# Gated layer, second pass: block sums move from GpSimd to VectorE, and one of them into the first pass

## The chip, the cores and the metric

One core of one Trainium2 chip. The time is the device time of one execution of the whole kernel in microseconds (us); lower is better. The engines are TensorE (PE in the rows; PEld is its weight load), VectorE (DVE), ScalarE (ACT), GpSimd (POOL) and SyncE (SP), which issues most of the DMAs.

## The reference, cut to what matters

Linear attention over 8 batches of 576 tokens gives a table of 4608 tokens by 512 features. A mixture of experts (one expert per token) works on it, and then the gated layer, which is the part that the change touches:

```python
rms = np.sqrt(np.mean(x * x, axis=-1, keepdims=True) + 1e-06)
xn = x / rms * rms_g                      # 4608 x 512
g = xn @ w_gate                           # 512 x 1536
silu = g * (1.0 / (1.0 + np.exp(-g)))
val = xn @ w_val                          # 512 x 1536
return (silu * val @ w_out).astype(np.float32)   # w_out: 1536 x 512
```

## The kernel before

The kernel runs attention, routing, experts and the gated layer one after the other, with some overlap. Only the gated layer matters here. It works on nine groups `j` of 512 tokens, in two passes, and each matrix product is done on 2x2 blocks with seven block products instead of eight (Strassen's scheme in Winograd's form); values are split into an upper and a lower half in 16 bits, and each block product is three 16-bit products.

**First pass** (`gated`, the loop over `j`). It computes u = silu(g) * val, transposed, and stores it to a scratch tensor `uscr` in DRAM as four blocks of 1536 columns for each group. Group 0 is computed plainly, in twelve chunks of features (`gate_chunk`: L1462 and L1463 make the product, L1465 stores it). Groups 1 to 8 go by `gate_group(j, i, more)`, three parts `i` each. A part makes seven block products for the gate (m = 0) and then seven for the value (m = 1), 12 matmuls each. In m = 1, `last` multiplies a block of the value by the finished block of the gate on VectorE (L1433) and issues its store on SyncE (L1434); the four blocks come in the order (2,2), (1,1), (2,1), (1,2). Between products, `more()` places pieces of the next group's preparation in program order: `in_gather` (four indirect DMAs issued by GpSimd, L1237), `in_rows` (the norm), `in_blocks` (four differences of blocks on GpSimd, L1291, splits on ScalarE and VectorE, L1300 and L1301, and transposes issued by SyncE, L1302). During group 0 the sums of the gate and value weights are made too (`all_sums`: VectorE L1347, GpSimd L1348 to L1351).

**Second pass** (`out_group(j)`). `out_load(j)` fetches the four blocks of u of a group from `uscr` into `ob[j % 2]` (768 KB each, SyncE). From them come the left operands of seven block products. Each operand is made by `out_left(j, n)`: ScalarE writes its upper 16-bit half (L1523) and VectorE the lower one (L1524), into one of five slots `os`. Four of the operands need sums of blocks, written in place by `out_sum`: t2 = t0 - t2 and t3 = t3 - t2 and t0 = t3 + t0 on GpSimd (L1511, L1513, L1515) and t1 = t1 - t3 on VectorE (L1517). `ahead(j, n)`, called behind product n, makes the operand of product n + 4, which may be one of the next group; with it come the sums that this operand or a later one needs, and behind operand 6 the loads of group j + 2.

`mul(n, p, first)` is one block product, 36 matmuls of 256 columns (L1557). The products 0 to 6 go into the PSUM banks a, d, g, b, e, a, e: product 6 adds onto bank e, which product 4 filled and which VectorE must have read before (L1572, the scaled add in `res` with u3). The results are added up with scaled adds on VectorE (L1589, L1590, L1572) and two scaled copies on ScalarE (L1582, L1596) and written out by `put`, four scatters of rows per group, indirect DMAs of GpSimd (L1575). The last of them, `left_put`, is issued in the next group.

All engines work their instructions in program order; the order is written out by hand, without a planner, in this part. At the junction of the passes, operands 0 and 1 of group 0 are made during group 8's last part; the slots 2 to 4 and `ob[1]` lie in memory that the first pass uses until its last store.

Of the kernel before, what the change touches and what calls it, by code (L numbers as in the profile page):

```python
# [9 lines left out]
F32 = mybir.dt.float32  # L10
# [6 lines left out]
ALU = mybir.AluOpType  # L17
# [6 lines left out]
NT, DM = B * S, H * D  # L24
# [109 lines left out]
class Kern:  # L134
# [1261 lines left out]
    def gate_group(self, j, i, more):  # L1396

        nc, v = self.nc, self.nc.vector
        x = self.xnT[j]

        def mul(p, k, r, first):
            n = 0
            for q in range(2):
                for dcl in range(2):
                    for w, y in ((0, 0), (0, 1), (1, 0)):
                        c = (y * 2 + dcl) * 256
                        nc.tensor.matmul(p[:, q * 256 : q * 256 + 256], self.left(k, self.m_, i, q, dcl, w), x[:, r, c : c + 256], start=first and n == 0, stop=n == 11, skip_group_check=True)  # L1407
                        n += 1

        out = {}  # L1410
        for m in range(2):
            self.m_ = m
            a, b, c, d = (self.ps.tile([128, 512], F32, tag="hy"[m], bufs=4, name=f"p{'abcd'[t]}{j}_{i}{m}") for t in range(4))
            mul(a, 0, 0, True)
            s1 = self.tmp(f"s{j}{i}{m}")
            nc.scalar.activation(s1, a, AF.Copy)  # L1416
            mul(b, 4, 1, True)
            u2 = self.tmp(f"u2{j}{i}{m}")
            v.tensor_tensor(u2, b, s1, ALU.add)
            mul(c, 5, 2, True)  # L1420
            u3 = self.tmp(f"u3{j}{i}{m}")
            v.tensor_tensor(u3, c, u2, ALU.add)
            mul(d, 3, 3, True)
            v.tensor_tensor(u3, d, u3, ALU.add)  # L1424
            c21 = self.tmp(f"c{j}{i}{m}")
            if m == 0:
                def last(o, t, key):
                    nc.scalar.activation(o, t, AF.Silu, scale=self.cg.bitcast(F32))  # L1428
                    out[key] = o
            else:  # L1430
                def last(o, t, key):
                    u, (r, h) = out[key], key
                    v.scalar_tensor_tensor(u, t, self.cv.bitcast(F32), u, ALU.mult, ALU.mult)  # L1433
                    nc.sync.dma_start(self.uscr[j, :, 2 * h + r - 3, i * 512 : i * 512 + 512], u)  # L1434

            last(u3, u3, (2, 2))
            more()
            mul(a, 1, 4, False)
            last(s1, a, (1, 1))
            more()  # L1440
            mul(c, 2, 5, False)
            v.tensor_tensor(c21, c, u2, ALU.add)  # L1442
            last(c21, c21, (2, 1))
            more()
            mul(d, 6, 6, False)
            v.tensor_tensor(u2, d, u2, ALU.add)
            last(u2, u2, (1, 2))

    def gate_chunk(self, j, fc):
        nc, v = self.nc, self.nc.vector  # L1450
        xT = self.xnT[j].rearrange("p a b -> p (a b)")[:, 0:4096].rearrange("p (c t) -> p c t", c=8)
        pg = self.ps.tile([128, 512], F32, tag="h", bufs=4, name=f"pg{j}_{fc}")
        pv = self.ps.tile([128, 512], F32, tag="y", bufs=4, name=f"pv{j}_{fc}")
        th, off = fc // 4, (fc % 4) * 128
        for p, o in ((pg, 0), (pv, 12)):
            k = 0
            for dc in range(4):
                for w, x in ((0, dc), (0, 4 + dc), (1, dc)):
                    nc.tensor.matmul(p, self.W[:, o + dc * 3 + th, w, off : off + 128], xT[:, x, :], start=k == 0, stop=k == 11)
                    k += 1  # L1460
        sg = self.tmp(f"sg{j}_{fc}")
        nc.scalar.activation(sg, pg, AF.Silu, scale=self.cg.bitcast(F32))  # L1462
        v.scalar_tensor_tensor(sg, pv, self.cv.bitcast(F32), sg, ALU.mult, ALU.mult)  # L1463
        r, c = (0, fc) if fc < 6 else (1, (fc - 8) % 6)
        nc.sync.dma_start(self.uscr[j].rearrange("p (h r) f -> p r h f", h=2)[:, r, :, c * 256 : c * 256 + 256], sg.rearrange("p (h t) -> p h t", h=2))  # L1465

    def b_part(self, a, i):
# [38 lines left out]

    def out_sum(self, j, n):

        g, t = self.nc.gpsimd, self.ob[j % 2]
        if n == 2:  # L1510
            g.tensor_tensor(t[:, 2], t[:, 0], t[:, 2], ALU.subtract)  # L1511
        elif n == 3:
            g.tensor_tensor(t[:, 3], t[:, 3], t[:, 2], ALU.subtract)  # L1513
        elif n == 4:
            g.tensor_tensor(t[:, 0], t[:, 3], t[:, 0], ALU.add)  # L1515
        else:
            self.nc.vector.tensor_tensor(t[:, 1], t[:, 1], t[:, 3], ALU.subtract)  # L1517

    def out_left(self, j, n):

# [5 lines left out]
    def ahead(self, j, n):  # L1526

        n += 4
        if n > 6:
            j, n = j + 1, n - 7  # L1530
        if j > 8:
            return
        if n == 0:
            self.out_sum(j, 2)
        elif n == 6:
            self.out_sum(j, 6)
        self.out_left(j, n)
        if n == 6 and j < 7:
            self.out_load(j + 2)
        if n == 1:  # L1540
            self.out_sum(j, 3)
            self.out_sum(j, 4)

    def out_group(self, j):

        nc, v = self.nc, self.nc.vector
        co = self.co.bitcast(F32)
        o = [self.ol.tile([128, 2, DM], F32, tag="o", name=f"o{j}_{h}", bufs=3) for h in range(2)]

        def mul(n, p, first, ss=range(2)):  # L1550
            slot = self.os[(7 * j + n) % len(self.os)]
            k = (0, 3, 2, 1, 4, 5, 6)[n]
            for s in ss:
                m = 0
                for c in range(6):
                    for w, y in ((0, 0), (0, 1), (1, 0)):
                        nc.tensor.matmul(  # L1557
                            p[:, s * 256 : s * 256 + 256], slot[:, w, c * 256 + s * 128 : c * 256 + s * 128 + 128], self.right(k, c, y),
                            start=first and s == 0 and m == 0, stop=m == 17, skip_group_check=True)
                        m += 1  # L1560
            if ss[0] == 0:
                self.ahead(j, n)

        def bank(nm, tag):
            return self.ps.tile([128, 512], F32, tag=tag, bufs=4, name=f"q{nm}{j}")

        def tmp(nm):
            return self.ol.tile([128, 512], F32, tag="ot", name=f"o{nm}{j}", bufs=4)

        def res(p, u, h, d, ss=slice(0, 2)):  # L1570
            pv, uv = (t.rearrange("p (s d) -> p s d", s=2)[:, ss] for t in (p, u))
            v.scalar_tensor_tensor(o[h][:, ss, 256 * d : 256 * d + 256], pv, co, uv, ALU.mult, ALU.add)  # L1572

        def put(h, s):
            nc.gpsimd.indirect_dma_start(  # L1575
                out=self.A["out"], out_offset=bass.IndirectOffsetOnAxis(ap=self.tokr[:, 4 * j + 2 * h + s : 4 * j + 2 * h + s + 1], axis=0),
                in_=o[h][:, s, :], in_offset=None, bounds_check=NT - 1, oob_is_err=False)

        a, d, g, b, e = bank("a", "h"), bank("d", "y"), bank("g", "h"), bank("b", "y"), bank("e", "h")
        mul(0, a, True)  # L1580
        s1 = tmp("s")
        nc.scalar.activation(s1, a, AF.Copy, scale=co)  # L1582
        mul(1, d, True)
        mul(2, g, True)
        if j:
            self.left_put()
        mul(3, b, True)
        u2, u3 = tmp("u"), tmp("w")
        v.scalar_tensor_tensor(u2, b, co, s1, ALU.mult, ALU.add)  # L1589
        v.scalar_tensor_tensor(u3, g, co, u2, ALU.mult, ALU.add)  # L1590
        res(d, u3, 1, 0)
        mul(4, e, True)
        res(e, u3, 1, 1)
        put(1, 0)
        mul(5, a, False)
        nc.scalar.activation(o[0][:, :, 0:256], a.rearrange("p (s d) -> p s d", s=2), AF.Copy, scale=co)  # L1596
        put(1, 1)
        if j == 8:
            for s in range(2):
                mul(6, e, False, (s,))  # L1600
                res(e, u2, 0, 1, slice(s, s + 1))
                put(0, s)
            return
        mul(6, e, False)
        res(e, u2, 0, 1)
        put(0, 0)
        self.left_put = partial(put, 0, 1)

    def gated(self):
# [191 lines left out]
```

## Time and profile before

| | before |
|---|---|
| median of 3 runs | 1410.31 us (1403.39 to 1411.08) |
| the profiled execution, its own time | 1409.75 us |
| its span, first to last instruction | 1408.0 us |
| busy share: TensorE, VectorE, ScalarE, GpSimd | 94%, 72%, 42%, 36% |
| second pass, first to last matmul | about 1119 to 1400 us of the span |

Busy shares are means over all stages. The chain of waits in the second pass runs through GpSimd's sums and scatters, VectorE's splits and stretches of TensorE. In the rows below, times are microseconds from the start of the span; "mean" durations are in nanoseconds; a bracket holds the idle time of the engine just before the instruction, and what ended it.

### The profile page before, as it was taken

Reading aid. Unit: us, or ns where it says so; the run is one execution under the profiler, and the core shown is the slowest. Engines: PE = TensorE matmul, PEld = TensorE weight load, DVE = VectorE, ACT = ScalarE, POOL = GpSimd, SP = SyncE. Lnnn points to the kernel's source line nnn. Section 1 sums busy time; section 2 is a strip of 40 time slices with the busy share of each in tenths; the row PEclk is TensorE's granted clock in tenths of the full one; section 3 lists DMA queues with packets and bytes.
Section 4 is the critical chain, followed back from the end, with each engine's and each line's share of the span. In section 5 each row is a group of like instructions: output and inputs, shape, how many; then the busy total and the mean of one; then the engine's idle time right before and its main releaser. Section 6 shows DMA issues by size and latency. Waiting matters only on the chain.

```text
span 1408.0 us, 32116 instructions
## 1 busy us (share of the span) xinstructions
PE 1318.0 (94%) x12387; PEld 1079.7 (77%) x12387; DVE 1019.0 (72%) x1940; ACT 597.5 (42%) x1053; POOL 512.6 (36%) x422
## 2 busy tenths in 40 slices
PE   8999589999989999996899999999999989988987
PEld 7888477777767766542788888888888878877876
DVE  6899967566787865199577777776666687677683
ACT  6888713122352455334533444443332253333341
POOL 5687552222122212076122312311210245555673
PEclk9999799999999999998999999999999999999999
DMA  8889296655677657321553433533525153444301
GB/s 304 283 297 285 83 258 159 145 138 152 169 188 168 180 117 204 65 68 35 130 119 100 121 93 92 139 98 106 143 83 180 53 195 131 143 159 153 128 31 61
DMA packets 174259, 202.56 MB, mean 144 GB/s; under 512 B 111204, under 2 KB 114312, under 8 KB 174032
## 3 DMA queue, kind: packets, MB, share of 16 engines
q1 hardware_dynamic: 163600, 171.27, 43.1%
q0 software_dynamic: 9904, 28.62, 6.3%
q8 instruction: 99, 1.62, 0.5%
q14 instruction: 128, 1.05, 0.3%
q10 hardware_dynamic: 528, 0.00, 0.0%
HBM read 115.66 MB, written 58.76 MB: 124 GB/s over the span
## 4 chain that ended last, share of the span: by engine, by line
PE 30%; issue 9%; DVE 8%; POOL 6%; DMA 3%; ACT 1%; POOLq 0%; ACTq 0%; DVEq 0%
PE pc L1407 8%; PE pd L1407 8%; PE pa L1407 8%; PE pb L1407 4%; DMA out<-o,tokr 2%; POOL out L1575 2%; POOL ob L1513 2%; POOL ob L1511 1%; DVE os L1524 1%; DVE S L1365 1%; DVE a L1347 1%; ACT os L1523 1%; DMA xnT<-xn 1%; DVE T L1365 0%; DVE ob L1517 0%
## 5 line engine op out<-in xcount | busy, mean ns | idle before, releaser
L1557 PEld LDWEIGHTS <-os 128*128 128x128 f16 x2268 | 225.8, 100 | 54.8 <-issue 18.3
L1407 PEld LDWEIGHTS <-W 128*128 128x128 f16 x2304 | 225.8, 98 | 44.0 <-ACT xn L1300 9.8
L1003 PE MATMUL hp<-xT,w1h 128*128 128x128 f16 x2368 | 204.4, 220 | 2.7 <-DMA xT<-xg 1.5
L1003 PE MATMUL hp<-xT,w1l 128*128 128x128 f16 x1184 | 201.8, 220 | 3.6 <-DVEq L1071 3.6
L1524 DVE TENSOR_TENSOR os<-ob,os 128x1536 f16<-128x1536 f32 x63 | 154.3, 2480 | 66.7 <-ACT os L1523 66.7
L1003 PEld LDWEIGHTS <-w1h 128*128 128x128 f16 x2368 | 184.2, 98 | 11.4 <-ACTq L1071 1.8
L1407 PEld LDWEIGHTS <-S 128*128 128x128 f16 x1728 | 169.4, 98 | 20.0
L1523 ACT ACTIVATE os<-ob 128x1536 f16<-128x1536 f32 x63 | 91.7, 1479 | 166.5 <-POOL ob L1511 71.0
L1407 PE MATMUL pa<-xnT,W 128*128 128x256 f16 x1152 | 142.7, 274 | 11.6 <-ACT xn L1300 9.3
L1003 PEld LDWEIGHTS <-w1l 128*128 128x128 f16 x1184 | 116.4, 98 | 4.5 <-DVEq L1071 4.4
L1020 PE MATMUL yp<-w2h,hh 128*128 128x512 f16 x296 | 112.1, 379 | 2.8 <-ACT wjunk L914 2.7
L1020 PE MATMUL yp<-w2l,hh 128*128 128x512 f16 x296 | 112.1, 379 | 2.8 <-DVE wI L142 2.4
L1010 DVE SCALAR_TENSOR_TENSOR hl<-hp,hh 128x512 f16<-128x512 f32 x74 | 51.1, 691 | 82.2 <-ACTq L1071 40.3
L1020 PEld LDWEIGHTS <-hh 128*128 128x128 f16 x592 | 56.4, 98 | 68.6 <-issue 8.5
L1575 POOL DMA_INDIRECT out<-o,tokr x36 | 59.5, 1653 | 101.5 <-DMA out<-o,tokr 71.0
L1557 PE MATMUL qe<-W,os 128*128 128x256 f16 x648 | 80.2, 286 | 17.1 <-DVE o L1572 16.9
L1009 ACT ACTIVATE hh<-hp 128x512 f16<-128x512 f32 x74 | 44.1, 596 | 109.4 <-PE hp L1003 98.3
L1428 ACT ACTIVATE u<-u,cg 128x512 f32<-128x512 f32 x48 | 34.7, 723 | 115.4 <-DVE u L1424 94.1
L1237 POOL DMA_INDIRECT yg<-yscr,slot x36 | 41.2, 1143 | 110.5 <-DVE c L1442 64.7
L1416 ACT ACTIVATE s<-pa 128x512 f32<-128x512 f32 x48 | 28.2, 588 | 109.1 <-PE pa L1407 109.1
L975 POOL DMA_INDIRECT xf<-fscr,tok x37 | 43.0, 1162 | 85.7 <-DVE scl L993 70.8
L975 POOL DMA_INDIRECT xg<-xscr,tok x37 | 43.9, 1185 | 81.9 <-DMA xT<-xg 76.1
(357 smaller groups left out, 2743.8 us busy)
## 6 DMA issues: line engine op xcount, KB each, us to landing
ob<-uscr SPq DMA_DIRECT2D x36, 768.0 KB, 6.4
uscr<-u SPq DMA_DIRECT2D x48, 256.0 KB, 2.0
yscr<-y SPq DMA_DIRECT2D x37, 256.5 KB, 3.3
kt<-in_kT SPq DMA_DIRECT2D x16, 576.0 KB, 5.6
q<-in_q SPq DMA_DIRECT2D x12, 768.0 KB, 6.0
xscr<-row SPq DMA_DIRECT2D x36, 256.0 KB, 4.5
vt<-in_v SPq DMA_DIRECT2D x8, 1024.0 KB, 8.7
w1s<-in_w SPq DMA_DIRECT2D x8, 1024.0 KB, 9.6
```

The source lines that it names most:

```text
L975: self.nc.gpsimd.indirect_dma_start(out=out, out_offset=None, in_=src, in_offset=bass.IndirectOffsetOnAxis(ap=self.tok[:, b : b + 1], axis=0),
L1003: nc.tensor.matmul(p[:, fc * 128 : fc * 128 + 128], w[:, dc, fs], xT[:, x, :], start=(fc == 0 and k == 0), stop=(fc == 3 and k == 11), ski ...
L1009: self.nc.scalar.activation(oh, p, AF.Relu)
L1010: self.nc.vector.scalar_tensor_tensor(ol, p, 0.0, oh, ALU.max, ALU.subtract)
L1020: nc.tensor.matmul(p, h[:, fc, :], w[:, fc, :], start=k == 0, stop=k == 23)
L1237: nc.gpsimd.indirect_dma_start(out=t[:, s, :], out_offset=None, in_=self.yscr[0:lim, :], in_offset=bass.IndirectOffsetOnAxis(ap=self.slot[ ...
L1407: nc.tensor.matmul(p[:, q * 256 : q * 256 + 256], self.left(k, self.m_, i, q, dcl, w), x[:, r, c : c + 256], start=first and n == 0, stop= ...
L1428: nc.scalar.activation(o, t, AF.Silu, scale=self.cg.bitcast(F32))
L1523: self.nc.scalar.activation(slot[:, 0], src, AF.Copy)
L1524: self.nc.vector.tensor_tensor(slot[:, 1], src, slot[:, 0], ALU.subtract)
L1557: nc.tensor.matmul(p[:, s * 256 : s * 256 + 256], slot[:, w, c * 256 + s * 128 : c * 256 + s * 128 + 128], self.right(k, c, y), start=firs ...
L1575: nc.gpsimd.indirect_dma_start(out=self.A["out"], out_offset=bass.IndirectOffsetOnAxis(ap=self.tokr[:, 4 * j + 2 * h + s : 4 * j + 2 * h + ...
```

## The change

The block t2 is now subtracted before it is stored: in the first pass GpSimd makes t0 - t2 from the two blocks of u that are at hand, and stores that. For groups 1 to 8 this is one subtraction of 128x512 for each of three parts, behind the multiply of block (1,2), for group 0 one of 128x256 in each of six chunks. In the second pass `out_sum(j, 2)` is gone, and the sums 3, 4 and 6 are all on VectorE. They stand directly behind the split of the operand before: sum 3 behind operand 2, sum 4 behind operand 3, sum 6 behind operand 5. In group 0 the operands of group 1 are made later than before: behind product 2 no operand is made for two products, and the last two of the four come behind the last scaled add. The buffers of the output tile `o` are taken in another order (h = 1 before h = 0), so that the tile written first in a group takes the buffer whose scatters are older.

```diff
                     v.scalar_tensor_tensor(u, t, self.cv.bitcast(F32), u, ALU.mult, ALU.mult)
+                    if key == (1, 2):
+                        nc.gpsimd.tensor_tensor(u, out[1, 1], u, ALU.subtract)
                     nc.sync.dma_start(self.uscr[j, :, 2 * h + r - 3, i * 512 : i * 512 + 512], u)
...
         r, c = (0, fc) if fc < 6 else (1, (fc - 8) % 6)
+        if r == 0:
+            nc.gpsimd.tensor_tensor(sg[:, 256:512], sg[:, 0:256], sg[:, 256:512], ALU.subtract)
...
-        g, t = self.nc.gpsimd, self.ob[j % 2]
-        if n == 2:
-            g.tensor_tensor(t[:, 2], t[:, 0], t[:, 2], ALU.subtract)
-        elif n == 3:
-            g.tensor_tensor(t[:, 3], t[:, 3], t[:, 2], ALU.subtract)
+        v, t = self.nc.vector, self.ob[j % 2]
+        if n == 3:
+            v.tensor_tensor(t[:, 3], t[:, 3], t[:, 2], ALU.subtract)
         elif n == 4:
-            g.tensor_tensor(t[:, 0], t[:, 3], t[:, 0], ALU.add)
+            v.tensor_tensor(t[:, 0], t[:, 3], t[:, 0], ALU.add)
         else:
-            self.nc.vector.tensor_tensor(t[:, 1], t[:, 1], t[:, 3], ALU.subtract)
+            v.tensor_tensor(t[:, 1], t[:, 1], t[:, 3], ALU.subtract)
...
-        if n == 0:
-            self.out_sum(j, 2)
-        elif n == 6:
-            self.out_sum(j, 6)
         self.out_left(j, n)
         if n == 6 and j < 7:
             self.out_load(j + 2)
-        if n == 1:
-            self.out_sum(j, 3)
-            self.out_sum(j, 4)
+        if n in (2, 3, 5):
+            self.out_sum(j, n + 1)
...
-        o = [self.ol.tile([128, 2, DM], F32, tag="o", name=f"o{j}_{h}", bufs=3) for h in range(2)]
+        o = {h: self.ol.tile([128, 2, DM], F32, tag="o", name=f"o{j}_{h}", bufs=3) for h in (1, 0)}
...
             if ss[0] == 0:
-                self.ahead(j, n)
+                if j or n < 3:
+                    self.ahead(j, n)
+                elif n > 4:
+                    self.ahead(j, n - 2)
...
         put(0, 0)
+        if j == 0:
+            self.ahead(j, 5)
+            self.ahead(j, 6)
         self.left_put = partial(put, 0, 1)
```

## Rows read from the trace of the kernel before

**Rows 1.** Stretches: length, busy us by engine, clock granted, DMA share, GB/s.
```profile
733.00:1119.00 386.00, 385.10 (x3518) 343.90 (x3517) 273.59 (x488) 146.81 (x296) 75.65 (x62) 1.00 0.41 113
1154.16:1181.67 27.51, 27.51 (x255) 24.66 (x252) 18.99 (x13) 8.10 (x7) 14.17 (x6) 1.00 0.44 154
1371.47:1400.00 28.53, 27.84 (x254) 24.55 (x251) 14.74 (x12) 5.72 (x5) 11.36 (x8) 1.00 0.14 56
1119.00:1400.00 281.00, 258.51 (x2270) 225.76 (x2268) 204.30 (x121) 98.55 (x79) 159.47 (x61) 0.96 0.35 125
```

**Rows 2.** The page's costliest groups: busy us, mean ns, idle before, releaser.
```profile
L1523 ACT ACTIVATE os<-ob 128x1536 f16<-128x1536 f32 x63 | 91.7, 1479 | 166.5 <-POOL ob L1511 71.0
...
L1557 PE MATMUL qe<-W,os 128*128 128x256 f16 x648 | 80.2, 286 | 17.1 <-DVE o L1572 16.9
```

**Rows 3.** Timeline of TensorE, two products 6: start, us.
```profile
1207.37 4.09 PE L1557 MATMUL qe<-W,os 128*128 128x256 f16 x36 [1.96 <-DVE o L1572]
...
1302.33 6.89 PE L1557 MATMUL qe<-W,os 128*128 128x256 f16 x36 [3.66 <-DVE o L1572]
```

**Rows 4.** Timeline of VectorE, from group 2.
```profile
1183.41 8.49 DVE L1524 TENSOR_TENSOR os<-ob,os 128x1536 f16<-128x1536 f32 x2 [8.52 <-ACT os L1523]
...
1195.93 1.76 DVE L1517 TENSOR_TENSOR ob<-ob 128x1536 f32<-128x1536 f32 x1
1199.33 3.43 DVE L1524 TENSOR_TENSOR os<-ob,os 128x1536 f16<-128x1536 f32 x2 [1.63 <-ACT os L1523]
...
1206.57 0.75 DVE L1572 SCALAR_TENSOR_TENSOR o<-qe,co,ow 128x512 f32<-128x512 f32 x1
```

**Rows 5.** Timeline of GpSimd, the same group.
```profile
1178.41 3.45 POOL L1511 TENSOR_TENSOR ob<-ob 128x1536 f32<-128x1536 f32 x1
...
1185.46 4.82 POOL L1515 TENSOR_TENSOR ob<-ob 128x1536 f32<-128x1536 f32 x1
1190.44 2.34 POOL L1575 DMA_INDIRECT out<-o,tokr  x1 [0.16 <-issue]
1194.76 2.00 POOL L1575 DMA_INDIRECT out<-o,tokr  x1 [1.98 <-DMA out<-o,tokr]
...
1209.54 0.98 POOL L1575 DMA_INDIRECT out<-o,tokr  x1 [7.60 <-DMA out<-o,tokr]
```

**Rows 6.** Timeline of all engines, at the junction of the passes.
```profile
1120.07 2.83 DVE L1433 SCALAR_TENSOR_TENSOR c<-c,cv,c 128x512 f32<-128x512 f32 x1
1122.43 3.76 POOL L1515 TENSOR_TENSOR ob<-ob 128x1536 f32<-128x1536 f32 x1
...
1123.53 3.20 DVE L1433 SCALAR_TENSOR_TENSOR u<-u,cv,u 128x512 f32<-128x512 f32 x1
1126.76 0.32 SPq L1434 DMA_DIRECT2D uscr<-u  x1
...
1128.83 4.23 ACT L1523 ACTIVATE os<-ob 128x1536 f16<-128x1536 f32 x3 [13.45 <-DMA uscr<-u]
```

**Rows 7.** Timeline of all engines, in the first pass.
```profile
844.19 1.50 POOL L1237 DMA_INDIRECT yg<-yscr,slot  x1 [10.79 <-DVE c L1442]
...
845.44 0.75 DVE L1433 SCALAR_TENSOR_TENSOR u<-u,cv,u 128x512 f32<-128x512 f32 x1
...
874.73 1.09 POOL L1291 TENSOR_TENSOR tb<-yg 128x512 f32<-128x512 f32 x1 [25.07 <-ACT yg L1263]
874.89 0.69 DVE L1422 TENSOR_TENSOR u<-pc,u 128x512 f32<-128x512 f32 x1
...
876.92 1.84 DVE L1433 SCALAR_TENSOR_TENSOR u<-u,cv,u 128x512 f32<-128x512 f32 x1
```

**Rows 8.** Timeline of all engines, from group 0 to group 1.
```profile
663.91 1.44 POOL L1291 TENSOR_TENSOR tb<-yg 128x512 f32<-128x512 f32 x1
...
665.56 0.74 DVE L1463 SCALAR_TENSOR_TENSOR sg<-pv,cv,sg 128x512 f32<-128x512 f32 x1
...
669.54 2.72 PE L1407 MATMUL pa<-xnT,W 128*128 128x256 f16 x12 [9.30 <-ACT xn L1300]
```

More of the change, by code (lines that the diff above doesn't have):

```diff
@@ L1577, in put @@
                 in_=o[h][:, s, :], in_offset=None, bounds_check=NT - 1, oob_is_err=False)
-        a, d, g, b, e = bank("a", "h"), bank("d", "y"), bank("g", "h"), bank("b", "y"), bank("e", "h")
+        a, d, g, b, e = (bank(nm, tag) for nm, tag in zip("adgbe", "hyhyh"))
         mul(0, a, True)
```

## The prediction

> **What bounds the kernel now.** I read the stretches of the second pass first, cut where a group's first matmul starts. There are nine groups, each of seven products of 36 matmuls. Group 1 takes 27.51 us with TensorE busy throughout, 3.93 a product: the floor. Nine floors are 247.6 us, and the stretch from 1119.00 takes 281.0 [rows 1]. So 33.4 us are lost: 7.6 in group 0, which ends at 1154.16, and 25.8 in the eight others. The first pass next to it has almost nothing to lose: 385.1 of 386.0 us [rows 1]. Whatever the change wins, it wins in the second pass.
>
> The grouped instructions then say who is late. TensorE waits for VectorE's scaled add (16.9 us, before product 6); ScalarE, which makes the upper half of each split, waits for GpSimd's block sums (71.0 for the first alone) [rows 2]; VectorE's lower half waits for ScalarE's upper one. A long gap also costs clock: over the pass the granted clock is 0.96 on average, in group 1 it is 1.00 [rows 1]. After 3.66 us of waiting one product took 6.89 us, part of it at 1.2 instead of 2.4 GHz; after 1.96 us it stayed at 4.09 [rows 3].
>
> VectorE in one group shows how GpSimd does it. Two splits took 8.49 us; undisturbed ones took 3.43 for two [rows 4]. They lie beside GpSimd's sums, the last of them 4.82 us long [rows 5]. From the last split of that group on, all is late, and the add that product 6 needs comes at 1206.57, where product 6 could have started at 1181.67 + 23.6 = 1205.3.
>
> GpSimd itself has the longest cycle: from the start of its first sum at 1178.41 to the end of the scatter after which the next group's first sum stands, 1209.54 + 0.98, it is 32.1 us. The three sums take it from 1178.41 to 1185.46 + 4.82, 11.9 us [rows 5]. While they are there, no group can be shorter than this in the long run.
>
> **The change part by part, second pass.** Removed: the three sums on GpSimd, 11.9 us a group. 32.1 - 11.9 = 20.2, so GpSimd drops below the floor. Added on VectorE: two sums at 1.76 us, the price of the one it already does [rows 4]. VectorE's work is then 7 x 1.75 (splits) + 3 x 1.76 + 5 x 0.75 = 21.3 us of 27.5. A split at 4.2, as the two of 8.49, no longer occurs, since no sum on GpSimd runs beside it.
>
> Order decides, so I follow the chain through VectorE and ScalarE. From the add before product 6 of one group to that of the next there lie, one behind the other: six lower halves of splits (10.5), three sums (5.3), four upper halves on ScalarE at 1.48 [rows 2] (5.9), four scaled adds at 0.75 [rows 4] (3.0), a ScalarE copy of 512 columns (0.5, a third of 1.48). That is 25.2, with some 0.6 us of hand-overs 25.8. It is 1.7 below 27.5, so a late chain catches up by 1.7 us a group, and in the steady state TensorE waits for nothing.
>
> The beginning isn't steady. Group 0's third product needs a split that begins when the last block of the first pass is stored. Now VectorE's last multiply there takes 3.20 us instead of 0.75, and an earlier one was held too, beside the sum on GpSimd; the store goes out at 1126.76 and the split starts at 1128.83 [rows 6]. Undisturbed, the two multiplies at 0.75 and the add between them, behind 1120.07, end at about 1122.3; the new subtraction on GpSimd (1.3, below) and the same 2.1 us from issue to the split give 1125.8, 3.0 earlier. From there the chain to the add before product 6 is five upper halves (7.4), four lower (7.0), three sums (5.3), the copy (0.5), four adds (3.0) and 0.8 for hand-overs: 24.0, so 1149.8. The waits of products 2 to 4 for their splits along this chain sum to some 4.4 us, so product 6 could begin at 1119.0 + 23.6 + 4.4 = 1147.0, and it waits 2.8 us. Group 0 ends at 1153.75, where now it is 1154.16: its loss stays at 7.2, because sums that ran beside the chain are now in it. Holding the splits of group 1 back until the loads have come costs VectorE nothing here: their place is in the next chain.
>
> In group 1 the chain starts when product 6 of group 0 is read, at 1154.7, and ends 25.8 later, at 1180.5. Product 6 is due at 1153.75 + 23.6 = 1177.3: a wait of 3.1. Group 1 ends at 1184.4, 2.7 later than now. In group 2 the add comes at 1206.3 and is due at 1208.0: no wait. Groups 2 to 7 at 27.51 put the start of group 8 at 1349.5; now it is 1371.47. Group 8 and the last scatters stay as they are: 22.0 us won.
>
> Off that goes the clock after the two waits of 2.8 and 3.1 us. They lie between 1.96 us (nothing lost) and 3.66 us (2.8 lost) [rows 3]; both ends are open, and I take 1.0 each: 20.0 us won.
>
> The scatters keep their queue alone. One takes 0.98 us with VectorE idle and 2.34 with it busy, and behind it about 2 us of waiting for the one before [rows 5]; four at 4.4 are 17.6 us, under 27.5. The Trainium skill (SBUF — State Buffer, section "SBUF: two separate sides") says that VectorE can starve GpSimd of the port that descriptors go through, and that each of the two holds the shared pair for a whole instruction. The lengthened scatters agree with the first half. By it the sum does not change while four scatters have 27.5 us.
>
> **First pass.** Added are 24 subtractions of 128x512 and six of 128x256 on GpSimd, each between a multiply and a store. GpSimd takes 1.09 [rows 7] to 1.44 us [rows 8] for the first kind, 1.27 in the middle; for the second I estimate 0.8, between half and the whole. Beside such an operation VectorE's multiply of two SBUF tiles took 1.84 us instead of 0.75 [rows 7]. Behind the subtraction VectorE next has adds that read PSUM, and such an add beside the same kind of operation stayed at 0.69 [rows 7]; this is the cover, and I cost the 24 at nothing. Without it they cost 24 x 1.27 = 30 us. On GpSimd the gathers of the next group (now at 844.19) wait for the multiply at 845.44 and the subtraction, some 3.3 us [rows 7]; the program has ScalarE read them behind eleven products of 1.3 us, so that is hidden too. On SyncE the store and the transposes behind it go 1.3 us later, where TensorE waits for none now.
>
> The six small ones fall where TensorE does wait: 9.30 us until 669.54 [rows 8]. Two of them lie before the sums that feed the first transposes, 2 x 0.8 = 1.6 us. The third difference (663.91) now queues behind chunk 8's subtraction, so behind the multiply of 665.56: 665.56 + 0.74 + 1.6 + 0.8 = 668.7, 4.8 us later [rows 8]. TensorE needs it third, so not all arrives; between 0 and 4.8 I take 2.3.
>
> **Sum.** 20.0 - 2.3 = 17.7 us less than the profiled execution's own 1409.75 us (span 1408.0): 1392. The median of the three runs is 0.6 above that execution, which changes nothing; one run was at 1403.39, so about 0.5% is what a measurement here can tell from no change.
>
> **Rivals.** (1) The waits of groups 0 and 1 shrink to what group 0 has at its start. Then 25.8 of 33.4 us go and the first pass costs nothing: 1384. For it: group 1 now runs at its floor. Against: three sums in a chain that had none beyond one.
>
> (2) The chain is longer than 27.5 us. It has 1.7 us in hand over some 18 links, 0.1 us each. At 28.5 each of groups 2 to 7 loses 1.0 and mostly stays out of the slow clock: 1398; at 29.5, with a slow clock in half of them, about 1408. Against: every link is an undisturbed row.
>
> (3) Slower: the scatters hold VectorE's two-input splits as the sums did. Four scatters at 2.0 us add 8 to the chain: 33.8, a loss of 6.3 in each of groups 2 to 8, 44 us: 1436. It decides from about 30.3 us on, where seven groups lose 17.7 + 2. Against it: VectorE's sum of 1195.93 stayed at 1.76 [rows 4], beside the scatter of 1194.76 that lasted 2.00 [rows 5]. The rule of the Trainium skill named above would give this, if a scatter counts as a GpSimd operation that reads SBUF; the trace disagrees.
>
> (4) Slower: the 24 subtractions are not covered, and each 1.27 us reaches TensorE: 1392 + 30 = 1422. For it: the stores' multiply is held in the shown row. Against: the first pass shows one wait of TensorE under 1 us in 386.
>
> **Chances.** Forecast 0.72, (1) 0.10, (2) 0.10, (3) 0.03, (4) 0.05. Faster by over 0.5% (below about 1403): 0.72 + 0.10 and half of (2), with a little off: 0.85; within: 0.07; slower: 0.08. The range 1383 to 1403 takes in (1), the clock at either bound, the first pass at either bound and the smaller half of (2).
>
> **What would show it.** Splits on VectorE at 1.75 us, 63 times, and no GpSimd arithmetic behind 1125; the first split after the junction at about 1125.8 on before's time plus the first pass's shift; waits of TensorE before product 6 in groups 0 and 1 of about 3 us and none behind them; groups 2 to 7 at 27.5. In the first pass TensorE's gaps between 660 and 682 grow by 2 to 3 us, and no new ones come. A recurring wait for the scaled add would make it wrong, and so would new waits in the first pass.

## The result, and the profile after

The changed kernel takes 1393.96 us (median of 5, 1386.25 to 1398.16) against 1407.42 us for the kernel before (5 runs, 1403.39 to 1411.08): a ratio of 0.9891, 95% interval 0.9849 to 0.9934. A second series, 6 runs against 11, gave 1400.59 against 1418.20, ratio 0.9857 (0.9823 to 0.9891). The profiled execution took 1388.32 us, its span is 1386.5; before it was 1409.75 and 1408.0.

From the page after: engines, then the costliest groups.

```profile
PE 1311.3 (95%) x12387; PEld 1078.4 (78%) x12387; DVE 1001.7 (72%) x1958; ACT 598.8 (43%) x1053; POOL 429.5 (31%) x425
...
L1526 DVE TENSOR_TENSOR os<-ob,os 128x1536 f16<-128x1536 f32 x63 | 110.4, 1756 | 56.1 <-ACT os L1525 56.1
L1525 ACT ACTIVATE os<-ob 128x1536 f16<-128x1536 f32 x63 | 92.7, 1480 | 124.5 <-DVE ob L1517 32.1
...
L1435 POOL TENSOR_TENSOR u<-s,u 128x512 f32<-128x512 f32 x24 | 30.5, 1270 | 245.2 <-DVE u L1433 226.6
...
L1554 PE MATMUL qe<-W,os 128*128 128x256 f16 x648 | 74.0, 273 | 6.0 <-DVE o L1572 5.2
```

Against [rows 2]: ScalarE now waits for VectorE's sums and no longer for GpSimd, and TensorE's wait for the scaled add fell from 16.9 to 5.2 us. All 63 splits on VectorE are at 1.76 us, and VectorE's busy time as a whole fell (1019.0 to 1001.7 us) although it got 18 sums more; its splits alone fell from 154.3 to 110.4 us.

Stretches after, as in [rows 1]; the first is the last 386 us of the first pass, then group 0, group 1, group 2, and the whole second pass to the end of the last matmul.

```profile
735.09:1121.09 386.00, 384.39 (x3509) 343.04 (x3507) 269.80 (x486) 146.00 (x295) 95.94 (x81) 1.00 0.40 112
1121.09:1155.01 33.92, 28.37 (x255) 24.32 (x252) 23.16 (x19) 12.69 (x10) 2.90 (x2) 1.00 0.59 217
1155.01:1185.07 30.06, 27.67 (x255) 24.65 (x253) 24.04 (x17) 11.49 (x10) 5.87 (x4) 1.00 0.38 141
1185.07:1212.58 27.51, 27.51 (x255) 24.66 (x253) 21.77 (x16) 12.63 (x10) 7.25 (x5) 1.00 0.45 155
1121.09:1378.54 257.45, 248.93 (x2270) 221.47 (x2267) 187.03 (x138) 100.77 (x79) 49.78 (x36) 1.00 0.37 137
```

Groups 2 to 7 are all at 27.51 us, TensorE busy throughout. What is left of loss stands in group 0 (6.4 us over the floor) and group 1 (2.6). Three rows from the changed kernel's timelines: the split that group 0's third product needs, then VectorE's scaled add before product 6 in groups 1 and 2.

```profile
1127.77 1.48 ACT L1525 ACTIVATE os<-ob 128x1536 f16<-128x1536 f32 x1 [10.33 <-DMA uscr<-u]
...
1180.34 0.74 DVE L1572 SCALAR_TENSOR_TENSOR o<-qe,co,ow 128x512 f32<-128x512 f32 x1
...
1205.74 0.74 DVE L1572 SCALAR_TENSOR_TENSOR o<-qe,co,ow 128x512 f32<-128x512 f32 x1
```

The waits of TensorE in this pass are few:

```profile
PE qe L1554 <- DVE o L1572: 5.2, 3, 2.4
PE qg L1554 <- DVE os L1526: 1.4, 1, 1.4
PE qb L1554 <- DVE os L1526: 0.9, 1, 0.9
PE qe L1554 <- DVE os L1526: 0.9, 1, 0.9
PE qg L1554 <- ACT os L1525: 0.2, 1, 0.2
```

Where the 21.5 us of span went, from the two traces: the second pass from its first matmul to the start of group 8 took 252.4 us (1119.04 to 1371.47) and takes 229.0 (1121.09 to 1350.13): 23.4 less. The first pass of the gated layer, from its first matmul (590.34, now 589.41) to the second pass, took 528.7 and takes 531.7: 3.0 more. What lies before it is 0.9 us shorter, and what lies behind the start of group 8 0.2.

### The profile page after: what moved, and what is told of

Read it like the earlier page. It is cut to its first block, busy times and chain, and to the rows that moved or that the text cites. A ratio compares the mean times of both kernels' runs of the same rounds, so it can differ in the third digit from the quotient of the medians.

```text
span 1386.5 us, 32151 instructions
## 1 busy us (share of the span) xinstructions
PE 1311.3 (95%) x12387; PEld 1078.4 (78%) x12387; DVE 1001.7 (72%) x1958; ACT 598.8 (43%) x1053; POOL 429.5 (31%) x425
## 4 chain that ended last, share of the span: by engine, by line
PE 43%; DVE 7%; issue 3%; DMA 2%; ACT 1%; POOL 1%; POOLq 0%; ACTq 0%; DVEq 0%
PE pc L1407 9%; PE pd L1407 8%; PE pa L1407 8%; PE pb L1407 4%; PE qe L1554 4%; PE qa L1554 3%; PE qg L1554 2%; PE qd L1554 2%; PE qb L1554 2%; DVE S L1365 1%; DVE a L1347 1%; DVE os L1526 1%; ACT os L1525 1%; DMA out<-o,tokr 1%; DMA xnT<-xn 1%
## 5 line engine op out<-in xcount | busy, mean ns | idle before, releaser
L1554 PEld LDWEIGHTS <-os 128*128 128x128 f16 x2268 | 221.6, 98 | 35.7 <-issue 5.7
L1526 DVE TENSOR_TENSOR os<-ob,os 128x1536 f16<-128x1536 f32 x63 | 110.4, 1756 | 56.1 <-ACT os L1525 56.1
L1525 ACT ACTIVATE os<-ob 128x1536 f16<-128x1536 f32 x63 | 92.7, 1480 | 124.5 <-DVE ob L1517 32.1
L1575 POOL DMA_INDIRECT out<-o,tokr x36 | 49.7, 1380 | 206.9 <-DVE o L1572 132.9
L1435 POOL TENSOR_TENSOR u<-s,u 128x512 f32<-128x512 f32 x24 | 30.5, 1270 | 245.2 <-DVE u L1433 226.6
L1554 PE MATMUL qe<-W,os 128*128 128x256 f16 x648 | 74.0, 273 | 6.0 <-DVE o L1572 5.2
L1407 PE MATMUL pd<-xnT,W 128*128 128x256 f16 x576 | 72.0, 276 | 3.3 <-ACT sg L1464 3.3
L1554 PE MATMUL qa<-W,os 128*128 128x256 f16 x648 | 73.7, 273 | 0.0
```

Source lines behind the costliest of these rows:

```text
L1435: nc.gpsimd.tensor_tensor(u, out[1, 1], u, ALU.subtract)
L1525: self.nc.scalar.activation(slot[:, 0], src, AF.Copy)
L1526: self.nc.vector.tensor_tensor(slot[:, 1], src, slot[:, 0], ALU.subtract)
L1554: nc.tensor.matmul(p[:, s * 256 : s * 256 + 256], slot[:, w, c * 256 + s * 128 : c * 256 + s * 128 + 128], self.right(k, c, y), start=firs ...
L1575: nc.gpsimd.indirect_dma_start(out=self.A["out"], out_offset=bass.IndirectOffsetOnAxis(ap=self.tokr[:, 4 * j + 2 * h + s : 4 * j + 2 * h + ...
```

## The experiments

The runs were made in three series, each on one chip and with 11 runs of the kernel before (median 1420.60, 1418.20 and 1411.45 us). So times are compared within a series, and ratios to the kernel before across them.

**One part alone: the stored difference.** The edits are the two subtractions in the first pass, and in `ahead`:

```diff
-        if n == 0:
-            self.out_sum(j, 2)
-        elif n == 6:
+        if n == 6:
             self.out_sum(j, 6)
```

> The kernel before with one part of the change alone: t0 - t2 is made and stored in the first pass; the sums 3 and 4 stay on GpSimd. Theory (the length of GpSimd's cycle sets the group): 32.1 us less one sum of 3.45 us is 28.6, so groups 1 to 7 of the second pass take 28.7 us on average (28.2 to 29.2; before 31.0), and with the first pass 3 us longer the whole is 13 to 16 us below before. Rival (GpSimd's sums hurt by holding VectorE's splits, not by their length): the two longest sums stay, so the groups stay at 30 to 31 us and the whole gains at most 5 us.

1400.59 against 1420.60 us, ratio 0.9867 (0.9839 to 0.9895). Its second pass, as stretches: group 0, then groups 1 to 7, then all.

```profile
1126.62:1161.99 35.37, 29.44 (x254) 25.23 (x252) 28.60 (x18) 14.06 (x11) 13.32 (x5) 0.90 0.55 201
1161.99:1354.56 192.57, 192.57 (x1766) 172.60 (x1764) 138.40 (x93) 79.88 (x63) 106.59 (x43) 1.00 0.39 137
1126.62:1382.98 256.36, 249.85 (x2270) 222.38 (x2267) 180.55 (x120) 99.66 (x79) 129.48 (x54) 0.99 0.38 137
```

192.57 is seven times 27.51: with one sum fewer on GpSimd all groups but the first are at the floor. That is better than the theory's 28.7, and the rival's 30 falls. The whole second pass is as short as in the changed kernel. So the steady state owes nothing to moving the sums 3 and 4 to VectorE, nor to the hold-back or the new order of the `o` buffers, which this kernel does not have; taking sum 2 off GpSimd was enough.

**Queue or port.** In that kernel, the sum's time is given back to GpSimd without its reads:

```diff
+        elif n == 0 and j:
+            x = self.xnT[8].rearrange("p a b -> p (a b)").bitcast(F32)
+            for k in range(2):
+                self.nc.gpsimd.memset(x[:, 1792 * k : 1792 * k + 1792], 0.0)
```

> The kernel before with the stored difference (sums 3 and 4 on GpSimd), and in place of sum 2, in groups 1 to 8, two fills of 128x1792 on GpSimd, which write unused memory and read nothing: about 1.75 us each by the fill of 584 columns in 0.59 us, 3.5 together, as long as the sum was. Theory (what counts is the length of GpSimd's queue): the cycle is 26.5 us (the shortest one seen with two sums) plus 3.5, groups 1 to 7 take 29 to 31 us, the whole is 10 to 25 us above the same kernel without the fills. Rival (what counts is that a sum reads two tiles beside VectorE's splits and holds them): groups 1 to 7 stay at 27.5.

GpSimd's timeline in it: the two fills and the two sums behind them, and the same fills a group later.

```profile
1244.73 3.15 POOL L1542 MEMSET xnT<- 128x1792 f32 x2
1247.82 3.45 POOL L1517 TENSOR_TENSOR ob<-ob 128x1536 f32<-128x1536 f32 x1
1251.34 3.44 POOL L1519 TENSOR_TENSOR ob<-ob 128x1536 f32<-128x1536 f32 x1
...
1274.31 3.16 POOL L1542 MEMSET xnT<- 128x1792 f32 x2
```

The cycle is 29.58 us, which is 26.5 plus the fills' 3.1, and five groups from 1216.66 on take 147.88, 29.58 each, with a wait of 1.9 us before product 6 in each; groups 1 and 2 are still at the floor. 1401.87 against 1411.45 us, 0.9924 (0.9894 to 0.9954), where the kernel without the fills has 0.9867: some 8 us, a little less than expected. The length of GpSimd's queue sets the group, the rival falls. VectorE is idle from 1243.9 to 1252.8 us, while the fills and the first sum run, so the fills don't act by holding its splits.

It isn't all. In the kernel before, GpSimd's cycle from the first sum of group 2, at 1178.41 [rows 5], to that of group 7 was 31.25 us on average:

```profile
1333.68 0.98 POOL L1575 DMA_INDIRECT out<-o,tokr  x1 [6.17 <-DMA out<-o,tokr]
1334.67 3.46 POOL L1511 TENSOR_TENSOR ob<-ob 128x1536 f32<-128x1536 f32 x1
```

That is 1.7 us more than with the fills. The sum is 0.35 us longer than the fills, and the sum t3 + t0 took 4.82 us before [rows 5] and takes 3.44 here, 1.4 less. Before, two splits ran beside GpSimd's sums (8.49 us [rows 4]); here only one does. That the splits lengthen this sum fits the rows, but was not tested by itself.

**The chain's margin.** The changed kernel, nothing added in the first pass, sum 2 on VectorE:

```diff
-        if n in (2, 3, 5):
+        if n in (1, 2, 3, 5):
             self.out_sum(j, n + 1)
```

> The changed kernel without the stored difference: nothing is added to the first pass, and sum 2 is made on VectorE too, behind operand 1. Theory (the chain through VectorE and ScalarE, 25.8 us, has 1.7 us in hand): with 1.76 us more, and with the upper half of operand 2 now behind a sum, it is 27.6 to 28.3 us, longer than the 27.5 of TensorE; a late chain never catches up, TensorE waits before product 6 in every group, groups 2 to 7 take 27.6 to 28.3 us. The first pass returns to its old length, 3 us less. The whole: 1 us less to 5 us more than the changed kernel. Rival (only VectorE's total work counts, 23.1 of 27.5 us): groups 2 to 7 stay at 27.5 and the whole is 3 us below the changed kernel.

1405.51 against 1420.60 us, 0.9894 (0.9867 to 0.9920). Two timelines, VectorE's scaled add before product 6 in groups 2 and 3, and TensorE's product 6 in groups 1 and 7.

```profile
1222.92 0.74 DVE L1570 SCALAR_TENSOR_TENSOR o<-qe,co,ow 128x512 f32<-128x512 f32 x1
1250.78 0.75 DVE L1570 SCALAR_TENSOR_TENSOR o<-qe,co,ow 128x512 f32<-128x512 f32 x1
```

```profile
1194.61 6.98 PE L1552 MATMUL qe<-W,os 128*128 128x256 f16 x36 [5.83 <-DVE o L1570]
...
1363.02 4.09 PE L1552 MATMUL qe<-W,os 128*128 128x256 f16 x36 [0.19 <-DVE o L1570]
```

The adds lie 27.86 us apart, in all of groups 2 to 7, inside the range that the theory gave. The first consequence that I drew from it was wrong: not every group waits. The chain uses 0.35 us a group, and TensorE waits again only in groups 6 and 7 (27.62 and 27.86 us), so the long wait of group 1 left some 1.4 us in hand, four groups' worth. The price is paid there: group 1 takes 36.4 us, where the changed kernel has 30.1. So groups 2 to 5 are at 27.51, as the rival said, but not for its reason.

**Group 0's beginning.** Operands 0 and 1 of group 0 a part earlier, its sums 3, 4 and 6 in the last part of the first pass:

```diff
-                    if j == 8 and i == 2 and k in (1, 3):
+                    if j == 8 and i == 1 and k in (1, 3):
                         self.ahead(0, next(first))
+                    if j == 8 and i == 2 and k in (0, 1, 3):
+                        self.out_sum(0, (3, 4, 0, 6)[k])
```

> The changed kernel with the sums 3, 4 and 6 of group 0 made in the last part of the first pass, and its operands 0 and 1 one part earlier; nothing else moves. Theory (group 0 waits for a chain of splits and sums, group 1 for the chain that starts when product 6 of group 0 is read): group 0 goes from 33.9 to 29.4 us (29 to 30.5), with a wait of 1.5 to 2 us before product 2 and none before products 3, 4 and 6; group 1 stays at 30 us with its wait of 2.4 before product 6. The whole: 4.5 us less. Rival (the lateness of group 1 is handed on from group 0): group 1 falls to 27.5 too, 7 us in all.

In this kernel operand 5 of group 0 is made from its block after sum 6, not before it, so it does not compute the same output; only its profile is read here. Groups 0 and 1:

```profile
1128.14:1157.27 29.13, 27.73 (x255) 24.51 (x253) 17.52 (x16) 12.37 (x10) 3.89 (x3) 1.00 0.67 262
1157.27:1189.00 31.73, 29.34 (x255) 25.51 (x253) 24.59 (x19) 12.70 (x10) 6.53 (x4) 0.95 0.34 125
```

Group 0 is at 29.13 as expected. Group 1 keeps its wait of 2.39 us, with 1.67 us of clock behind it. So its lateness isn't handed on from group 0. It fits the hold-back, which puts the chain of group 1 behind the end of group 0; the next run takes that out.

**The hold-back alone.** The changed kernel with `ahead(j, n)` behind every product, in group 0 too:

```diff
-                if j or n < 3:
-                    self.ahead(j, n)
-                elif n > 4:
-                    self.ahead(j, n - 2)
+                self.ahead(j, n)
...
-        if j == 0:
-            self.ahead(j, 5)
-            self.ahead(j, 6)
```

> The changed kernel without the hold-back of group 1's operands, nothing else. Theory (the same chain, only placed elsewhere): the add before product 6 of group 0 gets two splits in front of it, 3.5 us, so the wait there grows from 2.2 to 5.7 us and TensorE's clock falls behind it, 1.7 to 2.9 us; group 0 takes 37.4 plus the clock, 39 to 40.5 us. Group 1 then has 25.8 us for its chain and does not wait: 27.5. The second pass is 259.5 to 261.5 us. Rival (the hold-back was worth nothing): 257.4.

1402.65 against 1418.20 us, 0.9869 (0.9836 to 0.9902). Groups 0 and 1:

```profile
1133.51:1173.13 39.62, 30.75 (x254) 25.56 (x252) 27.90 (x22) 14.06 (x11) 3.90 (x3) 0.91 0.50 189
1173.13:1200.64 27.51, 27.51 (x254) 24.66 (x252) 20.37 (x16) 11.65 (x9) 4.26 (x4) 1.00 0.43 159
```

The wait before group 0's product 6 is 5.54 us, and group 1 has none: the chain is the same, only its place differs. The second pass is 260.6 us, where the changed kernel has 257.45 in its first profile and 260.7 in the repetition below, with medians of 1402.65 and 1400.59 us in one series. So the rival isn't ruled out: by itself the hold-back is worth between nothing and 3 us, as the clock falls.

**The first pass.** Group 0 without the six small subtractions, its sum 2 on GpSimd at the end of the first pass:

```diff
-        if r == 0:
-            nc.gpsimd.tensor_tensor(sg[:, 256:512], sg[:, 0:256], sg[:, 256:512], ALU.subtract)
...
+        if j == 0 and n == 0:
+            t = self.ob[0]
+            self.nc.gpsimd.tensor_tensor(t[:, 2], t[:, 0], t[:, 2], ALU.subtract)
```

> The changed kernel without the six small subtractions of group 0: its sum 2 is made on GpSimd at the end of the first pass, as before. Theory (the longer first pass comes from these six alone, through GpSimd's and SyncE's order from group 0 to group 1): the time from the first matmul of group 0's first pass to the first of its second pass goes from 531.7 back to 528.7 us (528.2 to 529.5). Rival (the 24 others cost it, or it is the scatter of runs): 531 to 532. The second pass is as in the changed kernel, 10 us over nine floors.

531.25 us: the theory fails. 1398.93 against 1420.60 us, 0.9844 (0.9820 to 0.9868). The start of group 1 in it, and then in the changed kernel, which has a wait of 1.02 us for a transpose before the second product:

```profile
681.82 2.72 PE L1407 MATMUL pa<-xnT,W 128*128 128x256 f16 x12 [10.53 <-ACT xn L1300]
684.33 2.77 PE L1407 MATMUL pb<-xnT,S 128*128 128x256 f16 x12
686.89 1.76 PE L1407 MATMUL pc<-xnT,S 128*128 128x256 f16 x12
690.07 1.47 PE L1407 MATMUL pd<-xnT,W 128*128 128x256 f16 x12 [1.42 <-ACT sg L1464]
```

```profile
668.97 2.72 PE L1407 MATMUL pa<-xnT,W 128*128 128x256 f16 x12 [9.83 <-ACT xn L1300]
672.71 1.47 PE L1407 MATMUL pb<-xnT,S 128*128 128x256 f16 x12 [1.02 <-DMA xnT<-xn]
674.01 1.47 PE L1407 MATMUL pc<-xnT,S 128*128 128x256 f16 x12
678.83 2.72 PE L1407 MATMUL pd<-xnT,W 128*128 128x256 f16 x12 [3.35 <-ACT sg L1464]
```

The wait for the transpose is there in all kernels with the small subtractions and in none without; but the waits of this stretch sum to 14.0 us in the kernel before, 15.3 in the changed one (14.3 in its repetition) and 14.3 here. Products that take 2.72 or 2.77 us instead of 1.47 run at a granted clock of 0.50, 1.2 GHz, and how many do differs from run to run. The kernel with all sums on VectorE has the first pass of the kernel before, and yet the same distance is 530.3 instead of 528.7 us, with waits only 0.5 us longer. The first 31 us of group 1, in the kernel before and in that one:

```profile
669.54:700.54 31.00, 26.26 (x220) 22.40 (x221) 17.41 (x34) 15.31 (x36) 4.85 (x5) 0.94 0.61 145
679.90:710.90 31.00, 27.03 (x207) 22.13 (x208) 16.53 (x33) 15.26 (x36) 4.84 (x5) 0.86 0.61 145
```

The granted clock is 0.94 in the one and 0.86 in the other (0.90 in the changed kernel, 0.86 in its repetition, 0.85 here). So of the 3.0 us some 1.6 are within what this start does by itself. The six profiles with all 30 subtractions on GpSimd lie between 531.5 and 532.1 us; this one and the put-together version below, both without the six, are at 531.25 and 531.8. A cost of the six above some 0.5 us is not seen.

The 24 others are seen in the last 386 us of the pass, where the clock is full: TensorE idles 0.90 us before [rows 1], 1.61 in the changed kernel, 1.94 here. They cost 0.7 to 1.0 us, not nothing. Are they better on VectorE?

```diff
-                        nc.gpsimd.tensor_tensor(u, out[1, 1], u, ALU.subtract)
+                        v.tensor_tensor(u, out[1, 1], u, ALU.subtract)
```

> The changed kernel with the 24 subtractions of 128x512 in the first pass on VectorE instead of GpSimd. Theory (they are covered on GpSimd, and VectorE has room too): the first pass from 50 us behind its second group's start to the end idles 0.9 us on TensorE, as in the kernel before, instead of 1.6; the last store leaves 0.6 us earlier. The whole: 1 us less, at most 2. Rival (VectorE is near its limit there, and 24 x 0.75 us more reach TensorE): 5 to 18 us more.

Both were off. The distance is 533.5 us, 1.5 to 1.9 more than in the two profiles of the changed kernel. TensorE idles 3.67 us in the last 386, a wait of 1.7 us for VectorE among it; 1395.26 against 1411.45 us, 0.9891 (0.9870 to 0.9911), where GpSimd's version has 0.9857 and 0.9891. TensorE's wait for VectorE's adds from 700 us on, then the same of the changed kernel:

```profile
PE pc L1407 <- DVE u L1422: 3.0, 2, 1.7
```

```profile
PE pc L1407 <- DVE u L1422: 0.9, 2, 0.7
```

**The same kernel again.**

> The changed kernel once more, beside the versions of this batch. Theory (TensorE's clock after a wait of 2.2 to 2.4 us is a matter of chance, and so is the clock after the 10 us gap at the start of group 1's first pass): the second pass takes 257.4 us where no clock is lost, 260.7 where both waits cost 1.67; the first pass, from the first matmul of group 0 to the second pass, 530.5 to 534. Rival (the earlier profile was of a kernel with fixed times): 257.4 and 531.7 again.

Product 6 of groups 0 and 1, behind the same waits as in the first profile, where both took 4.09 us:

```profile
1164.00 5.76 PE L1554 MATMUL qe<-W,os 128*128 128x256 f16 x36 [2.20 <-DVE o L1572]
...
1195.72 5.70 PE L1554 MATMUL qe<-W,os 128*128 128x256 f16 x36 [2.38 <-DVE o L1572]
```

The same two products as stretches, with a granted clock of 0.69 and 0.70, so in part at 1.2 GHz:

```profile
1164.00:1169.59 5.59, 5.59 (x36) 4.30 (x36) 3.28 (x2) 1.27 (x1) 2.62 (x2) 0.69 0.33 136
...
1195.72:1201.25 5.53, 5.53 (x36) 4.26 (x36) 3.64 (x3) 1.48 (x1) 3.23 (x2) 0.70 0.12 49
```

The second pass is 260.7 us, 3.2 longer with no wait longer: the waits agree to 0.02 us, the clock does not. The first pass is 532.0. Over the six profiles that have a wait of 2.20 to 2.39 us before product 6 of group 0 or 1, the product behind it was slowed six times out of ten.

**Put together.** Group 0's block stored whole, its sums 3 and 4 early (sum 6 in its old place), no hold-back:

> The changed kernel with three edits: group 0's block t2 is stored whole and its sum 2 made on GpSimd at the end of the first pass; the sums 3 and 4 of group 0 are made on VectorE in the last part of the first pass; the operands of group 1 are no longer held back. Theory (what is left of loss is the chain of sums in group 0, and in group 1 the chain that starts late because its operands were held back): group 0 29.1 us, group 1 27.5, all others as now, the second pass 250.1 us, 7.3 below the changed kernel's shortest, and the first pass 1 us less; 8 us below the changed kernel (5 to 11). Rival (without the hold-back, group 0's adds wait for loads of group 1's blocks): group 0 stays at 33 us or more.

1391.08 us against 1400.59 for the changed kernel and 1418.20 for the kernel before, on the same chip; 0.9798 (0.9765 to 0.9830). Group 0, group 1, and the whole second pass:

```profile
1130.40:1159.24 28.84, 27.84 (x254) 24.56 (x252) 21.49 (x17) 13.13 (x11) 2.89 (x2) 1.00 0.66 247
1159.24:1186.75 27.51, 27.51 (x254) 24.66 (x252) 21.88 (x16) 12.36 (x10) 6.47 (x5) 1.00 0.43 155
1130.40:1380.21 249.81, 248.24 (x2270) 221.71 (x2267) 182.29 (x134) 101.09 (x79) 47.96 (x36) 1.00 0.38 140
```

249.8 us where nine floors are 247.6. It beats both kernels: 9.5 us below the changed one.

The same with the sums 3 and 4 left on GpSimd in all groups:

> The kernel before with the stored difference for groups 1 to 8 only; group 0's sum 2 is made on GpSimd as before; operands 0 and 1 of group 0 are made one part earlier, so that its sums 3 and 4 on GpSimd run in the last part of the first pass. In all groups the sums 3 and 4 stay on GpSimd. Theory (one sum less is enough for GpSimd, and the loss at the junction is group 0's sums holding VectorE's last multiplies and its splits): group 0 29 to 30 us, all other groups 27.5, the second pass 250 to 251 us, the same as with the sums on VectorE. Rival (GpSimd's sums cost VectorE its ports at the junction wherever they stand): group 0 33 us or more.

1394.81 us, 0.9821 (0.9788 to 0.9853); second pass 249.84, group 0 28.85. The theory holds for the second pass, and the rival is seen in the first: GpSimd's sums of group 0 now hold VectorE's multiplies there (2.82 and 3.20 us, where the put-together version has 0.75), and one product waits 2.53 us for it:

```profile
1113.14 2.82 DVE L1433 SCALAR_TENSOR_TENSOR c<-c,cv,c 128x512 f32<-128x512 f32 x1
...
1116.61 3.20 DVE L1433 SCALAR_TENSOR_TENSOR u<-u,cv,u 128x512 f32<-128x512 f32 x1
```

So VectorE is the better place for these two sums, by some 2.5 us, for group 0's sake.

And the put-together version with the 24 subtractions on VectorE:

> The kernel with group 0's sums early and without the hold-back, and the 24 subtractions on VectorE too. Theory: both edits add, the second pass 249.2 to 249.9 us, the whole 0.5 to 1 us below the version with the subtractions on GpSimd, too little to be told apart by times. Rival: as for the subtractions on VectorE alone, 5 to 18 us more.

1381.35 against 1411.45 us, 0.9795 (0.9771 to 0.9819), the same as with them on GpSimd. In its profile the second pass is 249.2 us, 0.6 less, and the first 535.0, 3.2 more. The rival's 5 us and more do not show in the ratio, and no gain does either.

## Why the prediction was right

1392 us were forecast, 17.7 below the profile of before, and 1393.96 measured. The medians moved by 13.5 and 17.6 us, the profiles by 21.4. The second pass up to group 8 was to win 22.0 us without the clock and 20.0 with it; it won 23.4 in the first profile, where the clock stayed up, and 20.2 in the repetition, where it fell twice.

- **The floor and the steady state** came as stated: 27.51 us in groups 2 to 7, splits at 1.76, sums at 1.75, and no wait behind group 1. The chain was put at 25.8 us; from group 1 to group 2 the adds end 25.40 apart (1181.08 and 1206.48).
- **Why GpSimd had to be relieved** was right in kind, and three times too much was credited: I had all three sums to go for a cycle below the floor. The cycle with two sums was seen at 26.5 us (the kernel with the stored difference alone, from 1215.30 to 1241.82); one of them gone was enough. Simple subtraction, 32.1 - 3.45 = 28.6, misses this: 32.1 was the longest of five cycles that average 31.25, and the sum t3 + t0 is 1.4 us shorter once the first sum is gone. 31.25 - 3.45 - 1.4 gives 26.4.
- **The junction.** The split starts 6.7 us behind the start of the second pass, before 9.8: 3.1 earlier, 3.0 forecast. The waits of products 2 to 4 sum to 3.4 us, 4.4 forecast. Group 0 takes 33.9 (34.7 forecast) with 2.2 us before product 6 (2.8), group 1 30.1 (30.7) with 2.4 (3.1).
- **The clock** behind these two waits was put at 1.0 each. It is 0 in one profile and 1.67 and 1.61 in the next, behind the same waits; 1.0 is a fair mean of something that a single run does not have.
- **The first pass** is the step whose reasons failed while its size nearly held, by luck: 2.3 forecast, 3.0 in the profile. The six small subtractions were to cost all of it and cost no more than some 0.5; the wait that they bring for a transpose is given back by shorter waits behind it in most profiles. The 24 others were to cost nothing and cost 0.7 to 1.0. The rest goes with the clock behind a gap of 10 us, which differs as much between two kernels with the same first pass.
- **The rivals.** That the scatters hold VectorE did not happen: they run beside splits of 1.76 us. The rule of the Trainium skill (SBUF — State Buffer, section "SBUF: two separate sides") that VectorE and GpSimd each hold the pair of SBUF ports that they share for a whole instruction agrees with what two-input sums did at the junction (2.83 and 3.20 us for a multiply of 0.75 [rows 6]); the scatters did not hold VectorE so. A chain longer than 27.5 us came only with a fourth sum in it, at 27.86, and even then TensorE did not wait in every group.

## What to carry to other kernels

Count each engine's cycle per group, and the chain through the engines, against the floor of the bounding engine: one operation taken off the longest cycle may be all that is needed, and what lies below the floor can be moved about without a cost to the steady state. In a pipelined loop the first one or two groups have a chain of their own; here they held most of what was left, and work on data that is there early (group 0's sums) belongs ahead of the junction. A cycle only 0.35 us over the floor does not show for several groups, so the margin is read from the distance of the late engine's instructions and not from the waits.

## What the runs showed that I had not expected

TensorE's clock behind waits of 2.20 and 2.38 us fell in one run of the same kernel and stayed up in another (product 6 at 5.76 and 5.70 us, or 4.09), with the engine busy throughout before the wait; this alone makes 3.2 us between two runs of one binary. And a fill on GpSimd, which reads nothing, counted in its cycle like a sum of the same length, while VectorE's splits beside the rest stayed as they were (one of 3.58 us a group, with the fills and without).

GpSimd's cycle isn't only its work. Most of its idle time in the cycle before goes by waiting for a scatter to land before the next one; the longest such wait, 7.60 us [rows 5], falls into the loads of `ob`, at 229 GB/s. For group 8, when no loads run any more, the same wait is 2.02 us, and the cycle takes 25.2 us with all three sums (from 1334.67, above):

```profile
1358.52 1.35 POOL L1575 DMA_INDIRECT out<-o,tokr  x1 [2.02 <-DMA out<-o,tokr]
1359.88 3.45 POOL L1511 TENSOR_TENSOR ob<-ob 128x1536 f32<-128x1536 f32 x1
```

So the three sums alone do not make the cycle 32.1 us long, as the forecast had it. How much of it is due to the loads is not shown: no run moved them.
